# A new order table for attention, norm and the first feature tiles, with 45 dummy products in place of 95

## The chip, the cores and the metric

The kernel runs on one core of a Trainium2 chip. The metric is the device time of one execution, in microseconds (us). The engines are named as in the profile: PE is the tensor engine (PEld its weight loads), DVE the vector engine, ACT the scalar engine, POOL the GpSimd engine, and SP the engine that issues the loads and stores.

## The reference

Three layers follow each other for 2304 tokens (4 batches of 576) of 512 numbers. The attention is linear: q is normalised over each head's 64 numbers, k over all the tokens of its batch.

```python
q_s = np.exp(q - np.max(q, axis=-1, keepdims=True));  q_s = q_s / (np.sum(q_s, axis=-1, keepdims=True) + 1e-09)
k_s = np.exp(k - np.max(k, axis=2, keepdims=True));   k_s = k_s / (np.sum(k_s, axis=2, keepdims=True) + 1e-09)
kv = np.einsum('bhsd,bhse->bhde', k_s, v)             # 4 batches, 8 heads, 576 tokens, 64
x = np.einsum('bhsd,bhde->bhse', q_s, kv)             # then reshaped to 2304 x 512
xn = x / np.sqrt(np.mean(x * x, axis=-1, keepdims=True) + 1e-06) * rms_g
g = xn @ w_gate                                       # 512 -> 1536
x2 = (g / (1.0 + np.exp(-g)) * (xn @ w_val)) @ w_out  # 1536 -> 512
h = x2 @ w_in                                         # 512 -> 2048
y = (np.maximum(h, 0.0) + np.log1p(np.exp(-np.abs(h)))) @ w2_out   # 2048 -> 512
```

The weights of both dense layers arrive as float64 numbers.

## The kernel before

**Tiles and products.** Tokens come in six blocks of 384 (j = 0 to 5), hidden units in feature tiles of 128. Batches are cut into chunks of 128 tokens, three to a block; block 1 holds tokens of batch 0 and batch 1, so its attention output needs both. Each float32 product is three matmuls with float32r halves (`mm3`, L512 to L514: high by high, high by low, low by high), so a gate, value or output tile of one block is 12 matmuls of 384 columns. Each weight tile must first be turned from float64 words into those halves: an absolute value on ACT (CA, L213), a clamp (CL, L218), three bit operations on DVE (CD, L224, L228, L232), a cast on ACT (CC, L241) and a subtraction (CS, L246).

**Stages.** The first dense layer runs in groups of 3, 4 and 5 feature tiles; in a group each block takes its feature tiles one after the other, one *step* each: gate product G, Silu S (L593), value product V, product of both A (L605), its halves AH (L609) and AL (L613), output product O. Steps 0 to 14 are the first group for blocks 0 to 4. They, the attention, the norm and the conversion of the first weights are in the order table. From step 15 on code in loops sets the order; it is the same before and after the change.

**The order table.** `ORDER` is a string of operations. The program runs through it once; each operation emits its instructions to its engine, so each engine takes its share in the order of the table. An engine that waits holds up all that stands behind it on that engine alone. Where an operation can run on several engines, its last letter names one (V is DVE, P is POOL, A is ACT). The names are:

- LQ, LK, LX, LV, LW, LG: loads of q, k, v and the norm's factors; F.n: the load of weight tile n. All are issued by SP.
- K0 (maximum over tokens, L307), K1 (transposition, L315), KM (L321), K2 (spread over the partitions, L329), KS (subtraction, L336), KE (exponential, L341), K3 (products of k and v, PSUM tile `kvp`, L353 and L354), K4 (division, into `kvb`, L360 to L363): batch b, four heads at a time, K3.1.0 being batch 1's first four. K4.1.0 and K4.1.2 give batch 1's `kvb`.
- Q0 (L377), QS (L381), QE (L385), QR (L390 to L392), QM (L398): softmax of q; T (L406) and TC (L414): its transposition on PE and the copy to `qT_t`.
- X0.j.m: attention output of block j, a quarter m (L437); SQ its square (L442), XG its product with the norm's factor (L451, L453), XS sums of squares (L457), X1 (L464), XD (L469), XP (a power, L475) and X2 (L481) the root mean square, spread over the partitions, X3 (L485) the division; HH (L501, L503) and HL (L509) the halves that the gate product takes.
- E: copy of a block's finished output of the group (L564, L566).
- B.n: n *dummy* products (`busy`, L575) of a tile of zeros called `warm`, whose result nobody reads. A call is two records in the trace.

**Banks.** Of PSUM's eight banks, operations of the listed part other than G, V, O and B take spare ones in table order: five at first, two from the first gate product on (`bank`, `give`). A bank comes back when its last reader has been emitted.

Of the kernel before, what the change touches and what calls it, by code (L numbers as in the profile page):

```python
# [26 lines left out]
K0.0.0.1 LQ.0.1 B.2 LW.0 K0.0.1.1 QS.0.0.0.P B.1 QE.0.0.1 B.2 LV.0.4.8 K0.0.2.2 K1.0.0 B.1 QE.0.0.0 B.4 KM.0.0
K1.0.2 QR.0.0.0 K2.0.0 B.1 LQ.0.2 B.2 KM.0.2 QM.0.0.0.P B.1 QR.0.0.1 K2.0.2 B.1 F.3 B.1 T.0 KS.0.0 QM.0.0.1.P F.1
B.1 TC.0.A B.2 F.0 B.1 T.1 Q0.0.1 F.2 KE.0.0 B.3 LQ.1.0 B.1 KS.0.2 B.1 QS.0.1.0.P TC.1.A F.5 K3.0.0 F.4 QS.0.1.1.P
QE.0.1.0 F.7 KE.0.2 B.1 QR.0.1.0 B.1 F.8 B.3 LV.1.0.4 QE.0.1.1 Q0.0.2 K3.0.2 QM.0.1.0.V QS.0.2.0.P QR.0.1.1 T.2 MX.1  # L30
QE.0.2.0 B.1 K4.0.2 B.1 QM.0.1.1.P TC.2.A LK.1.2.2 B.2 CA.1 LX.1 B.1 QR.0.2.0 X0.0.3 CL.1.P F.6 X0.0.2 SQ.0.3 K4.0.0
LK.1.0.2 CA.0 B.2 LV.1.4.8 QM.0.2.0.V XG.0.3.A X0.0.0 SQ.0.2 CL.0.V X0.0.1 CA.3 CD.1.0 XS.0.2.3.P CD.0.0 SQ.0.0 B.1
CL.3.V B.1 SQ.0.1 B.1 CD.1.1 B.1 XG.0.0.A B.1 XS.0.0.1.P LW.1 B.1 Q0.1.0 CA.2 B.2 LQ.1.2 XG.0.2.A B.1 XS.0.0.2.P B.2
XG.0.1.A CL.2.V B.2 CD.1.2 B.1 QS.1.0.0.P X1.0 CD.2.0 CC.1 CD.3.0 B.2 QS.1.0.1.P XD.0 CA.4 B.1 CD.3.1 B.2 CD.0.1 B.2
CL.4.P QE.1.0 B.1 CD.3.2 B.1 LQ.1.1 B.2 CD.0.2 B.1 CC.3 B.2 QR.1.0 CA.7 B.1 XP.0 B.2 CC.0 B.2 CS.1.P CA.8 X2.0
CD.4.0 T.3 X3.0.0 T.4 TC.3.A CS.0.P QM.1.0.0.V B.1 TC.4.A B.2 CD.4.1 T.5 CL.8.P B.1 X3.0.1 B.2 HH.0.0.V B.1 X3.0.2
B.1 HH.0.1.A B.1 HL.0.0.V B.1 HH.0.2.A B.1 X3.0.3 B.1 HL.0.1.P G.0.0 K0.1.2.2 HH.0.3.A HL.0.2.P G.0.1 CA.5 CD.4.2
K1.1.2 HL.0.3.P G.0.2 KM.1.2 CC.4 CD.2.1 K2.1.2 CS.3.P CA.6 G.0.3 K0.1.0.2 V.0 CS.4.P KS.1.2 S.0 CL.6.P K1.1.0 G.1.0
KM.1.0 A.0 G.1.1 CD.2.2 K2.1.0 CL.5.P G.1.2 CD.6.0 KE.1.2 KS.1.0 G.1.3 V.1 CC.2 TC.5.A CD.6.1 CS.2.P AH.0.A Q0.1.2
KE.1.0 K3.1.2 Q0.1.1 QS.1.2.0.P CD.5.0 QS.1.1.0.P CD.6.2 K3.1.0 LV.2.4.8 K4.1.2 S.1 AL.0.V X0.1.2 MX.2 QM.1.0.1.V  # L40
QE.1.2.0 O.0 A.1 LV.2.0.4 CC.6 K4.1.0 AH.1.A CS.6.P SQ.1.2 CD.5.1 XG.1.2.A X0.1.0 CL.7.V CD.5.2 AL.1.P X0.1.3 SQ.1.0
CD.7.0 LK.2.2.2 CC.5 G.2.0 XG.1.0.V LQ.2.0 SQ.1.3 G.2.1 CS.5.P CD.7.1 XG.1.3.A G.2.2 LK.2.0.2 CD.8.0 X0.1.1 LW.2
CD.7.2 XS.1.2.3.P O.1 LX.2 CD.8.1 SQ.1.1 CC.7 QS.1.1.1.V XS.1.0.1.P XG.1.1.A CD.8.2 QE.1.1 CS.7.P XS.1.0.2.V G.2.3
T.6 CC.8 QR.1.1 X1.1 CS.8.P V.2 XD.1 S.2 QM.1.1.0.V XP.1 TC.6.A QM.1.1.1.P T.7 A.2 X2.1 TC.7.A AH.2.V X3.1.0 LQ.2.1
AL.2.P T.8 X3.1.1 TC.8.V O.2 X3.1.2 HH.1.0.V X3.1.3 HH.1.1.A HL.1.0.V HL.1.1.P X0.2.0 HH.1.2.V E.0.0.A E.0.2.V
HH.1.3.A X0.2.1 HL.1.2.V E.0.1.A HL.1.3.V G.3.0 SQ.2.0 SQ.2.1 E.0.3.V G.3.1 XG.2.1.A XS.2.0.1.V G.3.2 XG.2.0.V
X0.2.3 Q0.2.0 G.3.3 SQ.2.3 V.3 XG.2.3.A K0.2.2.2 S.3 QS.2.0.0.P QS.2.0.1.P Q0.2.1 X0.2.2 F.9 K1.2.2 SQ.2.2 G.4.0 A.3
QS.2.1.1.P G.4.1 XG.2.2.V G.4.2 KM.2.2 XS.2.2.3.P G.4.3 K0.2.0.2 QE.2.0 K2.2.2 QS.2.1.0.P V.4 AH.3.A KS.2.2
XS.2.0.2.P S.4 AL.3.V K1.2.0 F.10 X1.2 A.4 O.3 XD.2 KM.2.0 XP.2 QR.2.0 QE.2.1 AH.4.A K2.2.0 CA.9 QR.2.1 G.5.0
QM.2.0.0.P KE.2.2 G.5.1 G.5.2 CL.9.P CA.10 KS.2.0 T.9 G.5.3 V.5 AL.4.V QM.2.0.1.P CL.10.V TC.9.V S.5 QM.2.1.0.P  # L50
LQ.3.0 CD.10.0 O.4 A.5 QR.1.2.0 KE.2.0 QM.2.1.1.V X2.2 K3.2.2 AH.5.A X3.2.0 AL.5.V X3.2.1 LQ.3.1 HH.2.0.V O.5
LV.3.4.8 K4.2.2 HH.2.1.A HL.2.1.P X3.2.2 HL.2.0.V HH.2.2.A X3.2.3 T.10 E.1.2.A G.6.0 HL.2.2.V E.1.1.A QM.1.2.0.P
LK.3.2.2 TC.10.A HH.2.3.V G.6.1 Q0.3.0 T.11 HL.2.3.P K3.2.0 TC.11.V Q0.3.1 X0.3.3 MX.3 LV.3.0.4 QS.3.0.0.V G.6.2
QS.3.1.1.P SQ.3.3 G.6.3 QS.3.0.1.V V.6 CD.10.1 K4.2.0 LW.3 S.6 XG.3.3.V LX.3 X0.3.1 E.1.3.V LK.3.0.2 A.6 X0.3.0
CD.10.2 QE.3.0 G.7.0 E.1.0.V G.7.1 CC.10 QR.3.0 G.7.2 SQ.3.0 G.7.3 SQ.3.1 V.7 AH.6.A XG.3.1.A CS.10.V AL.6.P
XS.3.0.1.V QM.3.0.0.P XG.3.0.V X0.3.2 K0.3.2.2 S.7 T.12 SQ.3.2 O.6 TC.12.A K0.3.0.2 G.8.0 XS.3.2.3.V K1.3.0 A.7
XS.3.0.2.P G.8.1 KM.3.0 AH.7.A G.8.2 XG.3.2.V K2.3.0 AL.7.P G.8.3 KS.3.0 X1.3 QS.3.1.0.P S.8 V.8 XD.3 XP.3 X2.3
KE.3.0 A.8 O.7 X3.3.0 AH.8.V QE.3.1 X3.3.1 AL.8.P CD.9.0 HH.3.0.A X3.3.2 K3.3.0 QR.3.1 O.8 HL.3.0.V X3.3.3 HH.3.1.V
K4.3.0 HH.3.2.A G.9.0 E.2.1.A HL.3.1.V K1.3.2 E.2.3.A T.13 KM.3.2 HH.3.3.A G.9.1 HL.3.2.V E.2.0.A T.14 TC.13.V
E.2.2.A G.9.2 TC.14.A CD.9.1 K2.3.2 HL.3.3.V X0.4.0 KS.3.2 QM.3.0.1.P G.9.3 SQ.4.0 V.9 XG.4.0.V CD.9.2 S.9  # L60
QM.3.1.0.V F.11 X0.4.1 A.9 G.10.0 QM.3.1.1.V G.10.1 KE.3.2 G.10.2 G.10.3 AH.9.A K3.3.2 CC.9 AL.9.P F.12 CS.9.P V.10
K4.3.2 S.10 SQ.4.1 CA.11 XG.4.1.V XS.4.0.1.P CL.11.V X0.4.3 CD.11.0 A.10 X0.4.2 SQ.4.3 CD.11.1 O.9 CA.12 XG.4.3.V
SQ.4.2 CD.11.2 XG.4.2.A XS.4.2.3.P CL.12.V CC.11 F.13 AH.10.V G.11.0 CD.12.0 AL.10.P XS.4.0.2.V G.11.1 CD.12.1
G.11.2 CS.11.P G.11.3 CD.12.2 X1.4 S.11 CC.12 V.11 XD.4 XP.4 F.14 CA.13 CS.12.P X2.4 A.11 T.15 CL.13.P X3.4.0 O.10
AH.11.A X3.4.1 TC.15.A HH.4.0.A X3.4.2 X3.4.3 HL.4.0.P CA.14 T.16 HH.4.1.V CD.13.0 T.17 HH.4.2.A HL.4.1.V AL.11.P
G.12.0 TC.17.A CD.13.1 G.12.1 CL.14.P TC.16.V O.11 CD.13.2 HL.4.2.V CC.13 F.15 HH.4.3.V CD.14.0 X0.5.2 E.3.0.A
CS.13.V E.3.2.A X0.5.3 HL.4.3.V E.3.3.A CD.14.1 SQ.5.2 G.12.2 SQ.5.3 G.12.3 CD.14.2 XG.5.2.A XS.5.2.3.P V.12 S.12
XG.5.3.V CC.14 F.16 E.3.1.A CS.14.V CA.15 G.13.0 A.12 X0.5.0 CL.15.V AH.12.A CD.15.0 X0.5.1 SQ.5.0 AL.12.V G.13.1
CD.15.1 SQ.5.1 O.12 XG.5.0.V XS.5.0.1.P CD.15.2 XS.5.0.2.P XG.5.1.V CC.15 F.17 G.13.2 CS.15.V X1.5 G.13.3 XD.5 XP.5
V.13 S.13 X2.5 A.13 G.14.0 X3.5.0 G.14.1 AH.13.V HH.5.0.A G.14.2 X3.5.1 G.14.3 HL.5.0.P AL.13.V HH.5.1.A V.14 X3.5.2  # L70
# [833 lines left out]
```

## Time and profile before

| | |
|---|---|
| three runs | 974.17, 971.95, 974.18 us |
| median | 974.17 us |
| span of the profiled execution | 970.3 us |
| PE busy in the span | 950.6 us, 98% |
| DVE, ACT, POOL busy | 670.7, 513.5, 206.7 us |
| first gate product (step 0) starts | 48.09 us |
| step 15's first gate product starts | 205.84 us |

The span is the time from the first to the last instruction that the profile shows; the runs' times are some microseconds longer, with what lies around it. Times in the trace count from the start of the span. Busy time of PE is summed from modelled ends of pipelined matmuls and includes the dummy products, so it isn't useful work; starts of matmuls in a row tell what one costs. The granted clock of PE is given as a share of full speed, 1.00 being 2.4 GHz. An average over the span hides that the ordered part, the first fifth, and the rest have different limits; so the table of stretches is the view to begin with.

### The profile page before, as it was taken

The numbers are of one execution on the slowest core, as the hardware profiler recorded it, in microseconds if no ns is written. First come the engines' busy times: TensorE is split into PE (matmuls) and PEld (weight loads), VectorE is DVE, ScalarE is ACT, GpSimd is POOL, SyncE is SP. The second block draws the span as 40 slices with busy tenths as digits, with TensorE's granted clock in tenths as the row PEclk, the third lists the DMA queues.
The fourth block names the chain that finished last, engine by engine and source line by source line (L and its number), as shares of the span: only waits on it lengthen the run. The fifth ranks groups of instructions, "written<-read, shape, count | busy, mean of one in ns | idle before, by whom it ended". The sixth has DMA issues, their size and how long they took to land.

```text
span 970.3 us, 13904 instructions
## 1 busy us (share of the span) xinstructions
PE 950.6 (98%) x5374; PEld 895.4 (92%) x5374; DVE 670.7 (69%) x1160; ACT 513.5 (53%) x1014; POOL 206.7 (21%) x184
## 2 busy tenths in 40 slices
...
DMA packets 64162, 55.42 MB, mean 57 GB/s; under 512 B 25440, under 2 KB 58208, under 8 KB 64096
## 3 DMA queue, kind: packets, MB, share of 16 engines
...
q14 instruction: 24, 0.20, 0.1%
...
## 4 chain that ended last, share of the span: by engine, by line
PE 87%; DVE 8%; ACT 2%; issue 1%; POOL 1%; DMA 1%; SPq 0%; DVEq 0%; ACTq 0%
PE acc L514 11%; PE acc L513 11%; PE acc L512 11%; PE h L514 7%; PE h L512 7%; PE h L513 7%; PE v L512 5%; PE g L512 5%; PE v L514 5%; PE g L514 5%; PE g L513 5%; PE v L513 5%; PE kvp L353 2%; DVE km_t L307 2%; PE kvp L354 1%
## 5 line engine op out<-in xcount | busy, mean ns | idle before, releaser
L509 POOL TENSOR_TENSOR hl<-x,hl 128x384 fp32r<-128x384 f32 x68 | 70.1, 1031 | 618.9 <-ACT hl L501 536.4
L514 PE MATMUL h<-hl,w 128*128 128x384 f32 x384 | 129.5, 337 | 0.0
L512 PE MATMUL h<-hl,w 128*128 128x384 f32 x384 | 129.3, 337 | 0.0
L513 PE MATMUL h<-hl,w 128*128 128x384 f32 x384 | 128.9, 336 | 0.0
L850 DVE SCALAR_TENSOR_TENSOR u<-u,e 128x384 f32<-128x384 f32 x96 | 55.0, 573 | 82.8 <-ACT ln L847 82.8
L514 PE MATMUL acc<-w,hb 128*128 128x512 f32 x279 | 110.6, 397 | 0.2 <-DVE hb L843 0.2
L513 PE MATMUL acc<-w,hb 128*128 128x512 f32 x279 | 110.2, 395 | 0.0
L512 PE MATMUL acc<-w,hb 128*128 128x512 f32 x279 | 108.5, 389 | 0.0
L512 PE MATMUL g<-hl,w 128*128 128x384 f32 x288 | 99.9, 347 | 0.0
L763 DVE TENSOR_TENSOR a<-s,v 128x384 f32<-128x384 f32 x57 | 31.5, 552 | 97.5 <-PE v L514 97.5
L512 PE MATMUL acc<-h,w 128*128 128x384 f32 x288 | 97.3, 338 | 0.0
L513 PE MATMUL g<-hl,w 128*128 128x384 f32 x288 | 96.4, 335 | 0.7 <-DVE hl L509 0.7
L512 PE MATMUL v<-hl,w 128*128 128x384 f32 x288 | 97.0, 337 | 0.0
L514 PE MATMUL v<-hl,w 128*128 128x384 f32 x288 | 96.7, 336 | 0.0
L513 PE MATMUL v<-hl,w 128*128 128x384 f32 x288 | 96.6, 335 | 0.0
L513 PE MATMUL acc<-h,w 128*128 128x384 f32 x288 | 96.4, 335 | 0.0
L514 PE MATMUL g<-hl,w 128*128 128x384 f32 x288 | 96.3, 334 | 0.0
L514 PE MATMUL acc<-h,w 128*128 128x384 f32 x288 | 96.3, 334 | 0.0
L751 ACT ACTIVATE s<-g 128x384 f32<-128x384 f32 x57 | 28.1, 493 | 126.5 <-PE g L514 126.5
L765 ACT CAST h<-a 128x384 fp32r<-128x384 f32 x57 | 29.3, 514 | 116.3 <-DVE a L763 116.3
L837 ACT ACTIVATE e<-h 128x384 f32<-128x384 f32 x96 | 47.1, 490 | 75.6 <-PE h L514 75.2
L512 PEld LDWEIGHTS h<-hl,w 128*128 128x128 f32 x384 | 72.2, 188 | 4.1
...
## 6 DMA issues: line engine op xcount, KB each, us to landing
...
```

What stands on the lines that cost most here:

```text
L307: nc.vector.tensor_reduce(out=km_t[:, hs], in_=k_t[:, hs].rearrange("p h r d -> p h d r"), op=ALU.max, axis=AX.X)
L353: nc.tensor.matmul(out=a, lhsT=k_t[:, h, r, :], rhs=v_t[:, h, r, :], start=(r == 0), stop=False)
L354: nc.tensor.matmul(out=a, lhsT=k_t[:SX, h, R, :], rhs=v_t[:SX, h, R, :], start=False, stop=True)
L509: eng.tensor_tensor(out=t[:, 1], in0=src, in1=t[:, 0].bitcast(F32), op=ALU.subtract)
L512: nc.tensor.matmul(out=ps, lhsT=wh, rhs=xh, start=first, stop=False)
L513: nc.tensor.matmul(out=ps, lhsT=wh, rhs=xl, start=False, stop=False)
L514: nc.tensor.matmul(out=ps, lhsT=wl, rhs=xh, start=False, stop=last)
L751: nc.scalar.activation(out=s, in_=g_ps, func=AF.Silu)
L763: nc.vector.tensor_tensor(out=a, in0=s, in1=v_ps, op=ALU.mult)
L765: nc.scalar.copy(out=h[:, 0], in_=a)
L837: nc.scalar.activation(out=e, in_=ps, func=AF.Abs)
L850: nc.vector.scalar_tensor_tensor(out=u, in0=u, scalar=1.0, in1=e, op0=ALU.subtract, op1=ALU.subtract)
```

## The change

`ORDER` has 705 operations where it had 759; the operations that compute are the same. On each engine they stand in another order, movable ones go to other engines, and 45 dummy calls stand where there were 95. `x0g` no longer takes its bank handle out of the table of handles, so XG may stand ahead of SQ. Comments are gone, which makes line numbers of the code three smaller. Counts of instructions on DVE in the listed part, before and after: clamps L218 9 and 14, normalised q L398 8 and 2, XG L451 12 and 7, sums of squares L457 5 and 8, halves HH L503 9 and 7 and HL L509 14 and 8, AH L609 4 and 7, AL L613 7 and 9, result copies L564 4 and 6. ACT's reloads of its function table are 17 and 9.

```diff
 ORDER = """
-LK.0.1.1 LQ.0.0 MX.0 B.2 MK LK.0.0.1 B.1 LX.0 B.1 MV B.1 LK.0.2.2 B.1 LV.0.0.4 B.4 Q0.0.0 B.2 LG B.1 QS.0.0.1.P
+LQ.0.1 LQ.0.0 LX.0 Q0.0.1 QS.0.1.0.V MK QE.0.1.0 LQ.0.2 MX.0 Q0.0.0 LK.0.2.2 LK.0.1.1 QS.0.0.1.P Q0.0.2 QR.0.1.0
+QE.0.0.1 QS.0.0.0.P QM.0.1.0.P B.26 T.2 QE.0.0.0 LK.0.0.1 F.8 QS.0.1.1.P QR.0.0.1 K0.0.2.2 QR.0.0.0 QE.0.1.1 QR.0.1.1
...
-S.14 HL.5.1.P X3.5.3 O.13 HH.5.2.A A.14 HL.5.2.P HH.5.3.V AH.14.A HL.5.3.V AL.14.V
+HH.5.0.A AL.13.P HH.5.1.A A.14 HL.5.3.P HL.5.0.V CS.14.V HL.5.1.V AH.14.A AL.14.V O.13 F.16 F.17
 """
...
-        ps = xps.pop((j, m))
+        ps = xps[j, m]
```

PE at the start of the program, before; `busy` are the dummies, `qTp` is T's transposition, `kmT` is K1's and `kmb` K2's result:

```order
L575 MATMUL busy_115<-warm_80 128x128 x18
L315 MATMUL kmT_160<-ident_79,km_t_95 128x128 x2
L575 MATMUL busy_115<-warm_80 128x128 x5
L315 MATMUL kmT_171<-ident_79,km_t_95 128x128 x2
L329 MATMUL kmb_178<-ident_79,mx_169 128x128 x2
L575 MATMUL busy_115<-warm_80 128x128 x4
L329 MATMUL kmb_196<-ident_79,mx_187 128x128 x2
```

The same place after the change:

```order
L572 MATMUL busy_141<-warm_80 128x128 x26
L403 MATMUL qTp_168<-ident_79,qn_139 128x128 x4
L572 MATMUL busy_141<-warm_80 128x128 x2
L312 MATMUL kmT_197<-ident_79,km_t_95 128x128 x2
L403 MATMUL qTp_200<-ident_79,qn_192 128x128 x4
...
L326 MATMUL kmb_220<-ident_79,mx_207 128x128 x2
L403 MATMUL qTp_229<-ident_79,qn_205 128x128 x4
...
L312 MATMUL kmT_244<-ident_79,km_t_95 128x128 x2
```

The three transpositions of q in block 0 have moved ahead of and between those of k; more of the dummies stand at the very start and fewer behind.

PE at the first gate product (`g`), before; `ms` is X1, `rsb` X2, `qTp` are T.3 to T.5:

```order
L575 MATMUL busy_115<-warm_80 128x128 x14
L464 MATMUL ms_411<-ones_81,sq_t_97 128x1 x3
L575 MATMUL busy_115<-warm_80 128x128 x19
L481 MATMUL rsb_463<-ident_79,rs_422 128x128 x3
L406 MATMUL qTp_468<-ident_79,qn_330 128x128 x4
L406 MATMUL qTp_474<-ident_79,qn_364 128x128 x4
L575 MATMUL busy_115<-warm_80 128x128 x3
L406 MATMUL qTp_488<-ident_79,qn_481 128x128 x4
L575 MATMUL busy_115<-warm_80 128x128 x9
L512 MATMUL g_514<-hl_498,w_456 128x384
```

After; `kvp_512` is K3.1.2, `kvb0` and `kvb1` belong to batches 0 and 1, `xT` is X0.1.0 and X0.1.1:

```order
L351 MATMUL kvp_512<-v_t_94,k_t_93 64x65
L434 MATMUL xT_533<-qT_t_96,kvb0_98 128x192
L434 MATMUL xT_533<-qT_t_96,kvb1_99 128x192
L434 MATMUL xT_548<-qT_t_96,kvb0_98 128x192
L434 MATMUL xT_548<-qT_t_96,kvb1_99 128x192
L509 MATMUL g_570<-hl_536,w_297 128x384
L510 MATMUL g_570<-hl_536,w_297 128x384
```

Batch 1's K3 and two products of block 1 now stand ahead of the first gate product, where dummies stood; before, K3 of batch 1 came after the value products of step 1.

DVE around the second subtraction KS of batch 2 (`k_t` from `kmb`), before:

```order
L377 TENSOR_REDUCE qm_928<-qh_840 128x16
L605 TENSOR_TENSOR a_942<-s_924,v_909 128x384
L451 TENSOR_SCALAR xn_894<-xT_930,g_sb_83 128x384
L321 TENSOR_REDUCE mx_952<-kmT_934 128x2
L307 TENSOR_REDUCE km_t_95<-k_t_93 128x256
L336 TENSOR_TENSOR k_t_93<-k_t_93,kmb_960 128x1280
```

After; `bits` and `early` are weight tiles in conversion:

```order
L333 TENSOR_TENSOR k_t_93<-k_t_93,kmb_768 128x1280
L215 TENSOR_SCALAR bits_844<-bits_844 128x512
L454 TENSOR_TENSOR sq_t_97<-sq_t_97 128x384
L215 TENSOR_SCALAR bits_744<-bits_744 128x512
L374 TENSOR_REDUCE qm_862<-qh_727 128x16
L215 TENSOR_SCALAR early_434<-early_434 128x512
L221 TENSOR_SCALAR bits_844<-bits_844 128x512
L378 TENSOR_TENSOR qh_727<-qh_727,qm_862 128x8x64
L225 SCALAR_TENSOR_TENSOR bits_844<-raw_692,bits_844 128x512
L466 TENSOR_SCALAR rs_881<-ms_876 128x3
L221 TENSOR_SCALAR bits_744<-bits_744 128x512
L333 TENSOR_TENSOR k_t_93<-k_t_93,kmb_869 128x1280
```

Between the two subtractions of batch 2 now stand conversions of weights; before, batch 2's maxima and products of steps stood there.

## Rows read from the trace of the kernel before

**Rows 1.** Busy time per stretch: PE, PEld, DVE, ACT, POOL, then clock, DMA.

```profile
0.00:48.09 48.09, 42.18 (x326) 38.63 (x327) 36.82 (x66) 20.76 (x35) 28.16 (x31) 0.96 1.03 251
48.09:101.60 53.51, 47.74 (x305) 42.70 (x304) 50.55 (x69) 32.83 (x50) 34.03 (x28) 0.97 0.32 85
101.60:205.84 104.24, 100.31 (x668) 92.62 (x666) 86.81 (x150) 54.96 (x89) 43.32 (x38) 1.00 0.25 69
205.84:560.00 354.16, 354.16 (x2045) 354.16 (x2045) 193.35 (x364) 113.28 (x229) 0.00 (x0) 1.00 0.15 46
```

**Rows 2.** Single matmuls: start, duration, engine, line, tiles; steps 0 and 15.

```profile
48.09 0.43 PE L512 MATMUL g<-hl,w 128*128 128x384 f32 x1
...
205.84 0.33 PE L512 MATMUL g<-hl,w 128*128 128x384 f32 x1
206.01 0.33 PE L513 MATMUL g<-hl,w 128*128 128x384 f32 x1
```

**Rows 3.** Two heads of K3, from the same view.

```profile
60.86 0.68 PE L353 MATMUL kvp<-v_t,k_t 128*64 128x65 f32 x8
...
61.73 0.68 PE L353 MATMUL kvp<-v_t,k_t 128*64 128x65 f32 x8
```

**Rows 4.** K1, T, K2 and X0 between gate products, from the same view.

```profile
153.86 0.38 PE L315 MATMUL kmT<-ident,km_t 128*128 128x128 f32 x2
154.08 0.60 PE L406 MATMUL qTp<-ident,qn 128*128 128x128 f32 x4
154.43 0.42 PE L512 MATMUL g<-hl,w 128*128 128x384 f32 x1
...
156.01 0.61 PE L329 MATMUL kmb<-ident,mx 128*128 128x128 f32 x4
156.45 0.82 PE L437 MATMUL xT<-qT_t,kvb 128*128 128x192 f32 x4
156.97 0.48 PE L512 MATMUL g<-hl,w 128*128 128x384 f32 x1
```

**Rows 5.** X2 ahead of an output product, from the same view.

```profile
144.84 0.83 PE L481 MATMUL rsb<-ident,rs 128*128 128x128 f32 x6
145.42 0.43 PE L512 MATMUL acc<-h,w 128*128 128x384 f32 x1
```

**Rows 6.** Groups to 205.84: count | busy, mean ns | idle before; dummies.

```profile
L575 PE MATMUL busy<-warm 128*128 128x128 f32 x190 | 27.4, 305 | 1.0 <-DVE nhalf L526 1.0
```

**Rows 7.** Chain of waits: ten records of dummies at either clock.

```profile
10.46 2.07 PE busy L575 x10
...
27.44 1.12 PE busy L575 x10
```

**Rows 8.** Single instructions on DVE: its first one with its wait.

```profile
5.63 1.22 DVE L377 TENSOR_REDUCE qm<-qh 128x16 f32<-128x1024 f32 x1 [3.29 <-DMA qh<-in_q_dram]
```

**Rows 9.** Groups to 205.84 on DVE, as in rows 6.

```profile
L307 DVE TENSOR_REDUCE km_t<-k_t 128x256 f32<-128x1280 f32 x7 | 16.8, 2410 | 0.0
...
L336 DVE TENSOR_TENSOR k_t<-k_t,kmb 128x1280 f32<-128x1280 f32 x8 | 11.7, 1468 | 0.3 <-PE kmb L329 0.3
...
L605 DVE TENSOR_TENSOR a<-s,v 128x384 f32<-128x384 f32 x15 | 8.3, 550 | 7.4 <-PE v L514 7.2
...
L360 DVE TENSOR_SCALAR den<-kvp 128x2 f32<-128x2 f32 x8 | 1.3, 157 | 10.9 <-PE kvp L354 10.9
```

**Rows 10.** Groups to 205.84 on ACT and POOL, as in rows 6.

```profile
L246 POOL TENSOR_TENSOR w<-early,w 128x512 fp32r<-128x512 f32 x8 | 12.4, 1564 | 4.9 <-ACT w L241 4.9
...
L593 ACT ACT_TABLE_LOAD x9 | 11.5, 1283 | 3.2 <-PE g L514 3.0
...
L341 ACT ACTIVATE k_t<-k_t 128x1280 f32<-128x1280 f32 x8 | 10.2, 1270 | 1.4 <-DVE k_t L336 1.4
```

**Rows 11.** Two stretches of five microseconds, columns as in rows 1.

```profile
75.00:80.00 5.00, 2.37 (x16) 2.09 (x14) 5.00 (x5) 1.87 (x3) 3.60 (x3) 1.00 0.44 67
80.00:85.00 5.00, 4.63 (x22) 4.57 (x23) 3.53 (x7) 3.05 (x5) 3.67 (x3) 0.71 0.00 0
```

More of the change, by code (lines that the diff above doesn't have):

```diff
@@ L25 @@
 ORDER = """
-LK.0.1.1 LQ.0.0 MX.0 B.2 MK LK.0.0.1 B.1 LX.0 B.1 MV B.1 LK.0.2.2 B.1 LV.0.0.4 B.4 Q0.0.0 B.2 LG B.1 QS.0.0.1.P
[L27 to L70, printed above, removed]
@@ L71 @@
-S.14 HL.5.1.P X3.5.3 O.13 HH.5.2.A A.14 HL.5.2.P HH.5.3.V AH.14.A HL.5.3.V AL.14.V
+LQ.0.1 LQ.0.0 LX.0 Q0.0.1 QS.0.1.0.V MK QE.0.1.0 LQ.0.2 MX.0 Q0.0.0 LK.0.2.2 LK.0.1.1 QS.0.0.1.P Q0.0.2 QR.0.1.0
+QE.0.0.1 QS.0.0.0.P QM.0.1.0.P B.26 T.2 QE.0.0.0 LK.0.0.1 F.8 QS.0.1.1.P QR.0.0.1 K0.0.2.2 QR.0.0.0 QE.0.1.1 QR.0.1.1
+QM.0.0.1.P MV B.2 K1.0.2 T.1 QM.0.0.0.P KM.0.2 LW.0 K0.0.0.1 QS.0.2.0.P F.0 LV.0.0.4 B.2 K2.0.2 QM.0.1.1.P LV.0.4.8
+T.0 CA.8 CA.0 K0.0.1.1 KS.0.2 QE.0.2.0 LQ.1.0 B.2 K1.0.0 F.7 LQ.1.1 KM.0.0 CL.0.P TC.1.V QR.0.2.0 CD.0.0 B.2 K2.0.0
@@ new lines @@
+KE.0.2 TC.2.A CL.8.V KS.0.0 KE.0.0 B.1 K3.0.2 CD.0.1 TC.0.A CD.0.2 QM.0.2.0.P CC.0 K3.0.0 CD.8.0 Q0.1.0 K4.0.2 CD.8.1
+QS.1.0.1.P Q0.1.1 X0.0.2 F.3 K4.0.0 CA.7 F.4 QS.1.0.0.P QE.1.0 B.1 X0.0.0 CA.3 LK.1.0.2 LG SQ.0.2 QR.1.0 LX.1 LK.1.2.2
+CL.3.V CL.7.P X0.0.1 MX.1 CA.4 CD.7.0 SQ.0.1 XG.0.1.A CD.3.0 CL.4.V X0.0.3 CD.3.1 SQ.0.0 F.1 XG.0.3.A CD.4.0
+QM.1.0.1.V XS.0.0.1.P LV.1.0.4 T.3 SQ.0.3 XG.0.2.A XS.0.2.3.P LW.1 K0.1.0.2 LV.1.4.8 B.4 T.4 XS.0.0.2.P B.3 K1.1.0
+TC.4.A K0.1.2.2 B.1 X1.0 CA.1 K1.1.2 QM.1.0.0.P KM.1.0 XD.0 CL.1.V F.5 XG.0.0.A TC.3.A K2.1.0 XP.0 KM.1.2 T.5 K2.1.2
@@ new lines @@
+KS.1.0 X2.0 KE.1.0 QS.1.1.0.P CD.1.0 X3.0.1 QS.1.1.1.P TC.5.A KS.1.2 T.6 X3.0.0 CD.8.2 HH.0.1.A X3.0.3 KE.1.2 CS.0.P
+X3.0.2 F.6 CD.4.1 B.1 K3.1.0 HL.0.1.P CD.1.1 CD.3.2 QE.1.1 CD.1.2 K4.1.0 K3.1.2 X0.1.0 HH.0.0.A HL.0.0.P CA.6 CC.8
+CC.1 HH.0.3.A CL.6.V CD.7.1 X0.1.1 CC.3 LK.2.0.2 K4.1.2 SQ.1.0 CS.1.P SQ.1.1 QR.1.1 HL.0.3.P HH.0.2.A LK.2.2.2 G.0.0
+X0.1.2 SQ.1.2 MX.2 XG.1.2.A G.0.1 LX.2 X0.1.3 HL.0.2.V XG.1.3.A G.0.2 QM.1.1.0.V XS.1.0.1.V CD.4.2 CD.6.0 F.2 XG.1.0.A
+SQ.1.3 T.7 F.9 G.0.3 S.0 V.0 CS.3.V TC.6.A TC.7.A QM.1.1.1.P XS.1.2.3.V XS.1.0.2.P G.1.0 T.8 LQ.2.0 K0.2.0.2 G.1.1
@@ new lines @@
+CD.6.1 TC.8.A CD.7.2 CC.4 X1.1 G.1.2 CC.7 CS.4.P CD.6.2 XD.1 K1.2.0 CC.6 CS.7.P CS.6.P CA.5 G.1.3 A.0 XP.1 KM.2.0 S.1
+X0.2.0 Q0.2.0 CA.2 X0.2.3 F.10 V.1 AH.0.A K0.2.2.2 G.2.0 SQ.2.0 XG.2.0.A K1.2.2 XG.2.3.A SQ.2.3 X2.1 CL.2.V LQ.2.1
+LV.2.0.4 KM.2.2 XG.1.1.V A.1 G.2.1 CD.2.0 X0.2.1 CA.9 SQ.2.1 QS.2.0.0.P X3.1.0 AL.0.P QS.2.0.1.P XG.2.1.A G.2.2 X3.1.1
+XS.2.0.1.V G.2.3 HH.1.0.A CD.2.1 HL.1.0.P HH.1.1.A X3.1.2 X3.1.3 K2.2.0 HL.1.1.V LV.2.4.8 V.2 S.2 G.3.0 X0.2.2 AH.1.A
+HH.1.2.V HH.1.3.V QE.2.0 HL.1.3.P G.3.1 HL.1.2.V SQ.2.2 G.3.2 A.2 QR.2.0 G.3.3 V.3 CD.2.2 XG.2.2.A CS.8.P S.3
@@ new lines @@
+XS.2.2.3.V KS.2.0 QM.2.0.1.P CA.10 G.4.0 CL.10.V CC.2 XS.2.0.2.V T.10 LW.2 TC.10.A CL.9.V Q0.2.1 CL.5.V G.4.1 CD.10.0
+K2.2.2 G.4.2 QS.2.1.1.V X1.2 CD.10.1 XD.2 CD.9.0 CS.2.P KE.2.0 O.0 KS.2.2 QM.2.0.0.P AL.1.V KE.2.2 CD.5.0 CD.5.1
+QS.2.1.0.P G.4.3 CD.5.2 K3.2.0 AH.2.V LQ.3.0 K3.2.2 CD.9.1 A.3 CD.10.2 CD.9.2 V.4 K4.2.0 QE.2.1 AL.2.P CC.5 XP.2
+K4.2.2 S.4 CS.5.P T.9 X2.2 QR.2.1 G.5.0 X3.2.2 X3.2.0 X3.2.1 LK.3.0.2 TC.9.A LQ.1.2 QM.2.1.0.P O.1 Q0.3.0 G.5.1 T.11
+CC.9 G.5.2 MX.3 HH.2.1.A O.2 AH.3.V F.11 HL.2.1.P CS.9.P Q0.1.2 X3.2.3 LX.3 QS.1.2.0.V G.5.3 TC.11.A X0.3.3 HH.2.0.V
```

18 lines of the change are left out of this document (added).

## The prediction

> **What bounds the kernel now.** I read three things in this order: the table of busy time by stretch, the starts of single matmuls, and the groups by line. In the table [rows 1] the tensor engine (PE) is busy for all 354.16 us between 205.84 and 560: from the first product behind the ordered part (step 15) on, it has no gap to lose, and the change touches no instruction there. The part that the order table covers is different. Up to the first gate product at 48.09 [rows 2], PE's busy time is mostly dummy products on the `warm` tile; between 48.09 and 205.84 it shows 47.74 of 53.51 and 100.31 of 104.24 us. So I reduce the question to one number, **when does PE reach the first gate product of step 15, now 205.84** [rows 2]. What this moves, the end of the span moves. The span is 970.3 us, the median of the runs 974.17, so 3.87 us lie around the span; I take them as constant and forecast against 974.17.
>
> **What PE has to do in the ordered part.** Prices are from start to start, because ends are modelled. A matmul of 384 columns takes 0.173 us (205.84 to 206.01, [rows 2]), so a gate or value step of 12 takes 2.08, an output step as much. One head of K3 takes 0.87 (60.86 to 61.73, [rows 3]); a K3 has four, 3.48. From [rows 4]: a pair K1 0.22, a transposition T 0.36, K2 0.44, an X0 product some 0.5. X2 takes 0.58 [rows 5], X1 about the same. Thirty gate and value steps 62.4, fourteen output steps 29.1, eight K3 27.8, and 18 T, 24 X0, K1, K2, X1 and X2 some 30.8 make 150.1 us of useful work, the same before and after. Ahead of the first gate product stand 13.7 of it before (two K3, six T, four X0, X1, X2, K1 and K2 of batch 0) and 23.3 after, since K1, K2 and K3 of batch 1, a seventh T and two X0 of block 1 come ahead. So 136.4 are left behind that product before, 126.8 after. Before spends 205.84 − 48.09 = 157.75 on it: it loses 157.75 − 136.4 = **21.4 us** in waits and half-clock stretches. That loss is what a better order can win, and it is all that it can win.
>
> **Dummy products.** 95 calls become 45 (two records a call: 190 records, [rows 6]). They cost PE 27.4 us of busy time, but stand where it would wait. Ten records took 2.07 us at half clock and 1.12 at full clock [rows 7]. Taken out, they win nothing by themselves; I cost them at nothing as long as the engine that PE waits for, VectorE (DVE) as a rule, is what sets the next product's time. What they may cost is clock: see C.
>
> **The front, to the first gate product.** DVE's first instruction waits for a load, 3.29 us, and starts at 5.63 [rows 8]. After, the q half that it needs is the first load on the SP queue instead of the second; a slot there is some half a microsecond, so I take 5.1. From there to the second half-write of `kvb` for batch 1 (K4.1.0) stand 75 DVE instructions in the new order. Priced each at its form's mean in the trace to 205.84, they sum to 53.1: five `L307` maxima 9.7, four `L336` subtractions 5.9, five `L377` 5.5, the conversions of early weights 15.3, the rest 16.7 (the prices of the first two in [rows 9]). Those means overlap in part: all forms sum to 184.6, while the busy time in [rows 1] is 36.82 + 50.55 + 86.81 = 174.2, a factor of 0.944. So 53.1 × 0.944 = 50.1, and DVE is there at 55.2 if it waits for nothing in between. I take that, since matmuls, exponentials and POOL steps that feed it stand well ahead in the table; DVE did wait in this stretch before, mostly for K3's products (10.9 us over the ordered part, [rows 9]), so the bound above is 5.7 more (48.09 − 5.63 − 36.8 of busy time). The two X0 products of block 1 that come next in PE's order need K4.1.0: 2 × 0.58 = 1.2. The **first gate product comes at 56.4**, 8.3 later than before, with 9.6 more work done. With no loss at all behind it, step 15 would begin at 56.4 + 126.8 = 183.2.
>
> **Waits behind it.** I walked PE's, ACT's, POOL's and DVE's orders against each other with row means. Four places wait. (a) About 2.2 us at gate products of step 0 and X1.1, for K4.1.2, the low halves and a normalised q. (b) 1.5 at step 2's first gate product, which needs weight 6: DVE has finished its bits at 5.1 + 68.1 × 0.944 = 69.4, then an ACT cast, then two POOL subtractions at 1.56 each [rows 10] make 73, PE is there at 71.5. (c) 2.8 around the second K1 of batch 2, X2.1 and step 3's gate. (d) 5 us at K3 of batch 2: its `L336` subtraction stands behind six conversions and ends after 97.1 us of row means, that is 5.1 + 97.1 × 0.944 = 96.7; the exponential takes 1.27 [rows 10]; so K3.2.2 starts near 98.0 where PE is ready at 93. Together 11.5. Behind that the table keeps PE's inputs ahead of it in my walk, blocks 3 to 5 included.
>
> **What the walk can't see.** I add 5 us: about 3 for half clock behind waits, which halves PE's pace for some microseconds, and 2 for POOL and DVE disturbing each other and for DVE waiting on value products, which it did for 7.2 us before [rows 9]. 183.2 + 11.5 + 5 = 199.7, against 205.84: **6.1 us less, 974.17 − 6.1 = 968.0 us**.
>
> **Smaller edits.** DVE gives away six normalisations of q and seven low halves and takes clamps and two result copies; net some 3.4 us less over the ordered part by row means, in the sums above. ACT reloads its function table 9 times where the order had 17; each is 1.28 us [rows 10], 10 us of ACT time, hidden: ACT is busy 108.6 of 205.84 us [rows 1], and only a load directly ahead of a waiting product would count; I take 0 for it, bounds 0 and −3 (the 3.0 us it idled for gate products). POOL gains some 4 us by fewer clamps; it is at 105.5 of 205.84, and counts only where a weight's second half is late, (b). The fetch of weight 16 stands last on SP and waits for a conversion; nothing of the ordered part is behind it, and step 15's tiles are loaded before. The changed line in `x0g` (reading the bank handle without removing it) only permits XG ahead of SQ.
>
> **Rivals.** *B, the losses stay.* The walk sees waits of instructions but not all banks: the ordered part hands out spare banks in table order, two of them behind the first gate product, so a bank is one more thing to wait for. If as much is lost behind the first gate product as now, 21.4, step 15 begins at 183.2 + 21.4 = 204.6: 1.2 less, 973.0. For it: DVE's total work falls only by 3.4. Against it: the waits in (a) to (d) are half of 21.4 and I found no other.
>
> *C, the clock falls, and it is slower.* Now PE is granted only 0.71 of its clock in 80 to 85 us, right behind a stretch where it was busy for 2.37 of 5 us [rows 11], so the clock does fall here when PE has little to do. After the change 9 dummy calls stand between the last X0 product of block 0 and the first gate product, where 45 stood. If the four K3 ahead of it run at 1.2 instead of 2.4 GHz, they take 13.9 us more. DVE has other work beside the first two, so I count half of those as hidden: 13.9 − 3.5 = 10.4, and the first gate product comes at 66.8. With my own losses of 16.5, step 15 begins at 66.8 + 126.8 + 16.5 = 210.1, 4.3 late: 978.4; with the 21.4 of now, 983.3. It decides once the first gate product is later than 205.84 − 126.8 − 16.5 = 62.5. For it: the dummies, 38 records between X1 and X2 alone, were there for this. Against it: a K3 is a dense run of matmuls itself, and PE has more useful work in the front after the change.
>
> The Trainium skill, "TensorE: Matmul & The Clock Gate", section "Why this matters for your kernels", advises against gaps of the tensor engine between bursts of matmuls, as its clock then returns to half; that speaks against taking dummies out, and is rival C. The trace agrees as far as the 0.71 behind the half-idle stretch goes.
>
> *D, the walk as it is.* With no allowance step 15 begins at 194.7, 11.1 less: 963.1. It lies inside the range of the forecast.
>
> **How the numbers follow.** About 0.3%, 2.9 us, is what a measurement of this kernel can tell from no change: faster ends at 971.25, slower begins at 977.1. The forecast with D I give 0.62, B 0.20, C 0.18. A few hundredths of the forecast lie above 971.25 and of C below 977.1, which nearly cancel against B's own spread below: faster 0.63, same 0.20, slower 0.17. The range: below, D's 963.1 and 2 more for ACT's table loads, 961.0; above, over B to the near end of C, 978.5, which leaves out C's far part, about 0.10, and below some 0.07.
>
> **What will show it.** The first gate product near 56 (over 62: C); the start of step 15 near 200; the DVE sum ahead of K4.1.0 without waits of over 3 us; a wait of some 5 us at K3 of batch 2 near 95; the granted clock over 0.9 ahead of the first gate product; and from step 15 on, PE as dense as in [rows 1]. I would be wrong if DVE waits ahead of K4.1.0, if low halves or banks hold up steps 5 to 14, or if anything in the dense part moved.

## The result

| | before | after |
|---|---|---|
| runs | 974.17, 971.95, 974.18, 971.47 us | 965.27, 963.36, 964.65, 964.76 us |
| median | 973.06 us | 964.70 us |
| span of the profiled execution | 970.3 us | 963.5 us |
| first gate product | 48.09 us | 56.08 us |
| step 15's first gate product | 205.84 us | 199.07 us |
| DVE busy up to that | 174.17 us | 168.05 us |

The ratio is 0.9918, with an interval of 0.9903 to 0.9934: the change makes the kernel 0.7 to 1.0% faster. The span became 6.8 us shorter, and step 15 begins 6.77 us sooner, so all of the span's gain lies in the ordered part. The medians differ by 8.4 us; the runs of before lie 2.7 us apart, those of after 1.9.

The table of stretches of the kernel after; as in [rows 1] the columns are the stretch, the busy times of PE, PEld, DVE, ACT and POOL with their instructions, and PE's granted clock, DMA share and GB/s:

```profile
0.00:20.00 20.00, 14.88 (x85) 14.09 (x86) 13.99 (x25) 5.88 (x9) 11.61 (x19) 0.83 1.06 241
20.00:40.00 20.00, 14.21 (x123) 11.21 (x122) 19.57 (x34) 10.88 (x18) 10.36 (x10) 0.99 0.87 233
40.00:56.08 16.08, 15.49 (x124) 13.86 (x125) 14.88 (x23) 8.98 (x15) 8.87 (x8) 0.80 0.58 151
56.08:100.00 43.92, 39.19 (x240) 33.33 (x239) 43.54 (x66) 28.86 (x46) 22.90 (x21) 0.96 0.44 115
100.00:199.07 99.07, 97.68 (x629) 92.96 (x629) 76.07 (x136) 44.59 (x81) 44.98 (x42) 1.00 0.26 69
199.07:560.00 360.93, 360.93 (x2084) 360.93 (x2084) 198.62 (x374) 118.25 (x238) 0.00 (x0) 1.00 0.15 46
```

PE is dense from 199.07 on, as it was from 205.84 on. The new thing is DVE's column: from 20 us to 100 us it is full but for some 2 us. In the first 100 us it is busy for 91.98 us, against 85.77 before:

```profile
0.00:100.00 100.00, 83.78 (x568) 72.49 (x568) 91.98 (x145) 54.59 (x86) 53.74 (x55) 0.91 0.67 170
```

The same stretch of the kernel before:

```profile
0.00:100.00 100.00, 88.33 (x619) 79.73 (x620) 85.77 (x133) 52.02 (x83) 60.59 (x57) 0.97 0.67 166
```

What DVE waited for in that stretch, before (the waiting tile, the releaser, us in total, times, longest; the two longest of seven lines):

```profile
DVE den L360 <- PE kvp L354: 4.2, 2, 4.0
DVE qm L377 <- DMA qh<-in_q_dram: 3.3, 1, 3.3
```

and after (two lines of the program's start, the same in both, left out):

```profile
DVE qm L374 <- DMA qh<-in_q_dram: 2.6, 1, 2.6
DVE qm L374 <- DMA qx<-in_q_dram: 0.9, 1, 0.9
DVE xn L482 <- PE rsb L478: 0.6, 1, 0.6
DVE k_t L333 <- PE kmb L326: 0.5, 1, 0.5
```

The wait for K3's products is gone in that stretch. Between 10 and 90 us the list has two waits of DVE, 1.1 us in all. The chain of waits of the kernel after says the same: from 9.11 to about 90 us it runs over DVE, apart from 40.43 to 47.5 on PE and some 4 us on ACT near 78. Summed over its pieces between 9 and 90 us, DVE has 67.9 us of it and PE 6.5; before, DVE had 26.2 and PE 39.2. Its pieces where it passes to PE (start, us, what):

```profile
88.46 1.33 DVE sq_t L454
89.93 0.80 PE ms L461 x6
90.73 0.28 PE acc L509
```

That isn't for good: from 113.24 to 138.20 us the chain runs over DVE once more, which is busy for nearly all of that stretch. Two pieces of it, a maximum of batch 3 and the subtraction with which it hands over to PE, and then the stretch (columns as above):

```profile
120.97 2.08 DVE km_t L304
136.79 1.41 DVE k_t L333
```

```profile
113.00:138.20 25.20, 23.95 (x145) 22.73 (x143) 24.76 (x36) 15.17 (x24) 13.67 (x13) 1.00 0.24 63
```

### The profile page after: what moved, and what is told of

The parts are those of the page before. It is cut to its first block, busy times and chain, and to the rows that moved or that the text cites. A ratio compares the mean times of both kernels' runs of the same rounds, so it can differ in the third digit from the quotient of the medians.

```text
span 963.5 us, 13678 instructions
## 1 busy us (share of the span) xinstructions
PE 941.8 (98%) x5274; PEld 886.9 (92%) x5274; DVE 665.0 (69%) x1157; ACT 504.9 (52%) x1008; POOL 199.9 (21%) x185
## 4 chain that ended last, share of the span: by engine, by line
PE 86%; DVE 11%; ACT 1%; issue 1%; DMA 1%; SPq 0%; DVEq 0%
PE acc L511 12%; PE acc L510 12%; PE acc L509 11%; PE h L511 7%; PE h L509 7%; PE h L510 7%; PE g L509 5%; PE v L509 5%; PE g L510 5%; PE g L511 5%; PE v L510 5%; PE v L511 5%; DVE km_t L304 2%; PE kvp L350 1%; DVE k_t L333 1%; DVE qs L387 1%
## 5 line engine op out<-in xcount | busy, mean ns | idle before, releaser
L509 PE MATMUL h<-hl,w 128*128 128x384 f32 x384 | 129.3, 337 | 0.0
L509 PE MATMUL acc<-w,hb 128*128 128x512 f32 x279 | 108.5, 389 | 0.0
L509 PE MATMUL g<-hl,w 128*128 128x384 f32 x288 | 100.9, 350 | 0.0
L509 PE MATMUL v<-hl,w 128*128 128x384 f32 x288 | 97.7, 339 | 0.0
L509 PE MATMUL acc<-h,w 128*128 128x384 f32 x288 | 97.5, 338 | 0.0
L509 PEld LDWEIGHTS h<-hl,w 128*128 128x128 f32 x384 | 72.2, 188 | 4.1
```

Source lines behind the costliest of these rows:

```text
L509: nc.tensor.matmul(out=ps, lhsT=wh, rhs=xh, start=first, stop=False)
```

## The experiments

My theory is that VectorE's row of work in the first 90 us (up to X1 of block 2, `ms` in the lines above) sets when PE gets its inputs; the new order keeps VectorE fed there. The limit of 90 us leaves out the piece of the chain from 113 us on. (X1.2 belongs to block 2; the expectations call it batch 2's.) The rivals are that the new sharing among engines is the cause by itself, that dummies and PE's clock are, and that every wait of PE is a loss of its own.

### The two halves of the change alone

The order of after with the engines of before, and the order of before with the engines of after. Of the first, one line for example:

```diff
-G.0.2 QM.1.1.0.V XS.1.0.1.V CD.4.2 CD.6.0
+G.0.2 QM.1.1.0.V XS.1.0.1.P CD.4.2 CD.6.0
```

> The changed order, but every movable operation runs on the engine that it had before the change (101 operations differ). Theory order: VectorE's instructions and PE's products still stand in the new order, so most of the gain stays; VectorE has 2.9 us more work over the ordered part and 1.7 us more ahead of the first gate product: that product at 57 to 59, step 15's first at 200 to 203, about 966 to 970 us. Rival engines: the gain comes from sharing the work out anew, and with the old engines it is gone: 972 us or more, step 15 at 205 or later.

> The order of the kernel before with its 95 dummy calls, but every movable operation on the engine that the change gives it. Theory order: no more than 2.9 us of VectorE work less, in an order that was not made for it: 970 to 976 us, step 15 at 203 to 208, the first gate product near 48. Rival engines: most of the 8 us come, 964 to 967 us.

Measured: 981.3 us for the first (0.9% slower than before, 1.0072 to 1.0108) and 980.7 for the second (1.0066 to 1.0106). Neither theory had this: each half alone loses 8 us against before, and together they win 8. With the old engines the first gate product comes at 60.35, an output product of step 0 waits for a weight's second half on POOL, and step 15 begins at 214.79. With the new engines in the old order PE waits 3.4 us for a normalised q on POOL ahead of the first gate product, which comes at 53.36, and step 15 begins at 216.53. The waits of PE that lead the lists, of the first:

```profile
PE kmT L312 <- DVE km_t L304: 7.2, 2, 5.5
PE acc L511 <- POOL w L243: 4.4, 1, 4.4
```

and of the second, to its first gate product:

```profile
PE qTp L405 <- POOL qn L397: 3.4, 1, 3.4
```

DVE's busy time shows something more. Here are the stretches up to step 15, first of after, then of the second mix:

```profile
0.00:199.07 199.07, 181.46 (x1195) 165.45 (x1196) 168.05 (x280) 99.19 (x167) 98.72 (x96) 0.96 0.47 120
```

```profile
0.00:216.53 216.53, 197.18 (x1294) 180.20 (x1295) 173.46 (x280) 109.75 (x175) 99.69 (x96) 0.95 0.42 110
```

Both have 280 instructions of DVE, on the same engines, and the same forms; in the old order they take 5.4 us longer. So what the same instructions of DVE cost differs with the order. The granted clock up to step 15 differs too: 0.98 before, 0.96 after, 0.94 and 0.95 in the two mixes, so half-clock stretches have a share in their loss that isn't separated from the waits. The two mixes show that order and sharing are needed together; that a fuller row of VectorE is what the 6.8 us come from is read from the chains, and no run added to or took from VectorE's row in the order of before.

### Dummies

The changed kernel without any dummy; the changed kernel with 17 more; the kernel before with about half of each run of its dummies.

```diff
-... XS.0.0.2.P B.3 K1.1.0 TC.4.A ... K2.2.2 G.4.2 QS.2.1.1.V X1.2
+... XS.0.0.2.P B.3 B.13 K1.1.0 TC.4.A ... B.2 K2.2.2 G.4.2 QS.2.1.1.V B.2 X1.2
```

> The changed kernel without its 45 dummy calls. Theory order: VectorE sets the pace up to about 90 us, so a slower PE there costs only what lies on the chain: K3 of batch 0 and the products ahead of the first gate product at half clock, first gate product at 57 to 61, step 15 at 200 to 203, 965 to 969 us. Rival clock: PE at half clock sets the front, first gate product over 62.5, 970 us or more.

> The changed kernel with 17 dummy calls more: 13 ahead of K1.1.0, where PE waits 3.9 us and then runs at 0.50 of its clock, 2 ahead of K2.2.2 and 2 ahead of X1.2, where it waits 0.6 and 0.5 us and the output product behind runs at 0.66. Theory order with VectorE as the bound: the first spot gives at most the 1.06 us that VectorE waited there (44.3 and 47.0), the second up to 1.6 us: 962 to 964.5 us, first gate product 55 to 56. Rival clock: the whole 3.2 us of the first spot and the 1.6 come back: under 961 us. If dummies only delay: 965 or more.

> The kernel before, in its own order and with its own engines, with 45 dummy calls in place of 95, each run of them cut by about half. Theory order: dummies only fill waits of PE; fewer of them cost clock behind the waits in the front, 0 to 3 us: 972.5 to 975.5 us. Rival dummies delay: they stand in the way of real products and taking half of them out is a gain of more than 2 us: 970.5 us or less.

Measured: 966.45 us without dummies (interval of the ratio to before 0.9917 to 0.9953); the first gate product comes at 57.93, 1.85 later than in after, and step 15 1.81 later. With 17 more 963.18 (0.9890 to 0.9921), first gate product 54.68, step 15 at 196.84. Before with 45 calls stays where it was: 972.64, ratio 1.0005 (0.9996 to 1.0014). So going from 95 to 45 has no price by itself in the order of before. In the changed kernel all 45 are worth 1.8 us by the medians, and the 17 give 1.5, but both intervals overlap that of after (0.9903 to 0.9934); in the profiled executions it is 1.8 and 2.2 us of span. Two stretches of after:

```profile
40.00:44.00 4.00, 3.46 (x16) 3.33 (x17) 3.79 (x6) 1.14 (x3) 1.79 (x2) 0.50 0.85 155
...
90.00:95.00 5.00, 5.00 (x22) 4.75 (x23) 5.00 (x9) 0.24 (x1) 1.16 (x1) 0.66 0.36 105
```

and the same with 17 dummies more:

```profile
40.00:44.00 4.00, 3.31 (x30) 3.06 (x29) 3.90 (x6) 1.63 (x3) 2.65 (x4) 1.00 1.01 176
...
90.00:95.00 5.00, 4.30 (x40) 3.70 (x38) 5.00 (x9) 0.61 (x1) 1.07 (x1) 1.00 0.27 82
```

With the dummies the granted clock is 1.00 in both. At the first place the first gate product comes 1.4 us sooner; VectorE had only short waits there. Of this gain not all is sure: after and two kernels of the next sections that differ from it only further on have that product at 56.08, 56.20 and 57.10 in their traces; this kernel and two that differ from it only further on have it at 54.68, 54.78 and 56.34. At the second place the output product of step 0, which took 3.71 us (90.59 to 94.30) at 1.2 GHz, goes at 2.4 GHz.

### PE's waits against VectorE's row

Two operations move on VectorE, meant to end PE's two longest waits behind the first gate product, with no work added or removed.

```diff
-HH.0.3.A CL.6.V CD.7.1 X0.1.1 CC.3 LK.2.0.2 K4.1.2 ... QR.1.1 HL.0.3.P ... X0.1.3 HL.0.2.V
+HH.0.3.A K4.1.2 CL.6.V CD.7.1 X0.1.1 CC.3 LK.2.0.2 ... HL.0.3.P ... X0.1.3 HL.0.2.V QR.1.1
```

> The changed kernel with two operations moved on VectorE alone: K4.1.2 ahead of two conversions (CL.6, CD.7.1), and QR.1.1 behind the low half HL.0.2. VectorE does the same work; PE's two longest waits right behind the first gate product (X0.1.2 2.0 us and G.0.2 1.7 us too long) should go. Theory VectorE chain: VectorE works without a gap up to X1 of batch 2 at 90 us, so the 3.7 us that PE gains are given back ahead of that place: 963.7 to 965.5 us, within 1 us of the changed kernel, X1.2 at 89 to 90.5. Rival PE waits: each wait of PE removed is time gained: 961 to 962 us, step 15 near 195.5.

Then a maximum over tokens is done twice, once in batch 1 (near 38 us), once in batch 3 (near 119).

```diff
-XS.0.0.1.P LV.1.0.4 T.3 SQ.0.3 XG.0.2.A XS.0.2.3.P LW.1 K0.1.0.2
+XS.0.0.1.P LV.1.0.4 T.3 SQ.0.3 XG.0.2.A XS.0.2.3.P LW.1 K0.1.0.2 K0.1.0.2
```

> The changed kernel with one maximum of batch 1 (K0.1.0.2, 2.4 us on VectorE, starting near 38) done twice; the result is the same. Theory VectorE chain: the first gate product moves by 2.0 to 2.6 us to some 58.4 and step 15 by as much, to some 201.4: 966.5 to 967.3 us. Rival PE waits: it is partly hidden, under 1 us: 964.7 to 965.7 us.

> The changed kernel with one maximum of batch 3 (K0.3.0.2, 2.4 us on VectorE, near 119 to 121) done twice. Behind 95 us PE is nearly dense and VectorE has gaps. Theory VectorE chain up to 95 only: hidden but for 0 to 0.8 us: 964.5 to 965.5 us. If VectorE sets the pace here too: 966.5 to 967.3 us.

Measured: the first, 964.31 us, is within 0.4 of after. The edit ended one of the two waits, 1.7 us at X0.1.2; the other, for T.7's q, grew from 0.9 to 1.7. PE still reached V.0 at 62.65, 1.0 us sooner than in after (with the first gate product 0.7 later), but X1 of block 2 at 89.77, where after has 89.93: what PE had gained was given back there. Step 15 begins 0.96 us sooner; that was won behind X1 of block 2, where this execution was granted 1.00 of the clock in 90 to 95 us. The second, 967.55, is 2.85 more; the first gate product moves from 56.08 to 58.76, X1 of block 2 to 92.60, step 15 to 200.95. Both speak for VectorE's row up to 90 us, and against PE's waits as losses of their own. The third speaks against a limit to 90 us: it costs 2.5 us, at 967.21, where I expected under 0.8. In its trace step 15 is 2.33 us late, of which 0.69 was there at X1 of block 2 already, with the same code up to there. PE waits for the doubled maximum:

```profile
125.88 0.41 PE L312 MATMUL kmT<-ident,km_t 128*128 128x128 f32 x2 [2.11 <-DVE km_t L304]
```

In after that transposition starts without a wait, but the maximum had ended just ahead of it:

```profile
123.76 0.38 PE L312 MATMUL kmT<-ident,km_t 128*128 128x128 f32 x2
```

So a place with no wait in the trace need not have slack. VectorE is full there too, and this maximum is the piece at 120.97 us of the chain shown above, which runs on to T.13's wait at 138.33. What was wrong was my limit of 90 us, and that VectorE has gaps behind it: between 113 and 138 us it has next to none.

### Taking work from VectorE

If VectorE's row is the bound, less of it should help: four operations ahead of X1 of block 2 go to POOL where POOL is idle.

```diff
-QM.1.1.0.V ... CS.3.V TC.6.A TC.7.A QM.1.1.1.P ... XS.2.0.1.V ... XS.2.0.2.V
+QM.1.1.0.P ... TC.6.A TC.7.A QM.1.1.1.P CS.3.P ... XS.2.0.1.P ... XS.2.0.2.P
```

> The changed kernel with four operations of VectorE handed to POOL where POOL is idle: QM.1.1.0 (1.53 us on VectorE), CS.3 (0.68), XS.2.0.1 (0.55) and XS.2.0.2 (1.40); all stand ahead of X1 of batch 2. Theory VectorE chain: X1.2 comes 2 to 3.5 us sooner, near 87, and step 15 1 to 2.5 us sooner (other places bind behind it): 962 to 963.8 us. If something else than VectorE's amount of work sets X1.2, or POOL is too slow for it: 964.5 us or more.

Measured: 967.93 us in the median, 3.2 more than after, where 0.9 to 2.7 less was expected. Its twelve runs lie in two groups: six between 965.18 and 966.33, with 0.989 to 0.991 of the clock granted over the span (after has 0.989 to 0.993), and six between 969.54 and 972.4, with 0.981 to 0.986. So only about 1.3 us of the loss stand at the clock of after; the rest goes with a lower clock, and there is no trace of such a run. The profiled execution, 965.86, is of the first group: step 15 begins at 199.65, 0.58 later than in after, and X1 of block 2 starts at 90.25, no sooner. VectorE's instructions in after from 62.44 on (start, us):

```profile
62.44 0.55 DVE L454 TENSOR_TENSOR sq_t<-sq_t 128x384 f32<-128x384 f32 x1
62.91 0.68 DVE L229 SCALAR_TENSOR_TENSOR early<-early 128x512 int32<-128x512 int32 x1
63.51 0.41 DVE L221 TENSOR_SCALAR early<-early 128x512 int32<-128x512 int32 x1
```

and the same three in this kernel, with POOL beside them:

```profile
61.10 1.40 DVE L454 TENSOR_TENSOR sq_t<-sq_t 128x384 f32<-128x384 f32 x1
62.42 1.53 DVE L229 SCALAR_TENSOR_TENSOR early<-early 128x512 int32<-128x512 int32 x1
63.88 1.52 DVE L221 TENSOR_SCALAR early<-early 128x512 int32<-128x512 int32 x1
```

```profile
60.94 2.46 POOL L395 TENSOR_TENSOR qn<-qh,qs 128x512 f32<-128x512 f32 x2 [2.90 <-PE xT L434]
63.37 1.74 POOL L243 TENSOR_TENSOR w<-early,w 128x512 fp32r<-128x512 f32 x1
```

Three instructions that took 1.64 us take 4.45 while POOL does, among other things, the first two of the operations that VectorE was rid of; those had taken 2.21 us on VectorE. Near 77 us VectorE also waits 1.5 us for K1 of batch 2, which it doesn't in after. Up to step 15 VectorE has four instructions fewer, 4.2 us by their durations in after, and is busy for 167.80 us instead of 168.05: almost all of it came back as longer instructions. The Trainium skill, "SBUF — State Buffer", section "SBUF: two separate sides", says that the two engines share a pair of ports as an exclusive lock: where a GpSimd instruction meets a VectorE instruction in a two-port mode, or, if it reads SBUF, one with two inputs in SBUF, the one that starts first holds the pair for its whole instruction and the other blocks. The three durations agree with it: each instruction ends 0.3 to 0.6 us behind the end of one on POOL (at 62.08, 63.40 and 65.11). The third has one input only, and no run here shows its mode.

### One more wait, and all together

In after, T.13 waits ahead of V.8 for a bank that VectorE reads:

```profile
138.33 0.63 PE L403 MATMUL qTp<-ident,qn 128*128 128x128 f32 x4 [1.39 <-DVE k_t L333]
```

To the kernel with 17 dummies more I added the exchange of T.13 and V.8, and then also the four operations on POOL.

```diff
-T.13 X3.3.1 CA.13 E.1.0.A CL.13.P QE.3.1 V.8
+X3.3.1 CA.13 E.1.0.A CL.13.P QE.3.1 V.8 T.13
```

> The kernel with 17 dummies more (963.2 us), and T.13 behind V.8 instead of ahead of it on PE: T.13 waits 1.4 us for a bank until VectorE's subtraction for batch 3 has read it, and V.8 could run in that time. Theory bank wait is a loss of its own: step 15 1.0 to 1.5 us sooner, 961.5 to 962.5 us. If PE only waits elsewhere instead: 963 us or more.

> The changed kernel with 17 dummies more, T.13 behind V.8, and the four operations handed from VectorE to POOL together. If the three gains add: 959.5 to 961.5 us. If they share one limit: 962 us or more.

Measured: 962.83 us with the exchange (0.9891 to 0.9916), the fastest of all, and 967.21 with the four operations besides (0.9933 to 0.9967). The exchange gives 0.35 us in the median, less than its runs scatter; in the profiled executions step 15 begins 1.4 us sooner, but 1.1 of that was there at X1 of block 2, ahead of the exchange. VectorE is gone from the chain between 95 us and step 15, which now runs over PE, and yet little is won. That the bank's wait is a loss of its own stays open. The kernel with everything has three runs between 964.97 and 965.75, at 0.991 of the clock, and three between 968.67 and 970.62, at 0.984 to 0.989; either group is slower than the exchange alone, so the gains don't add. Its profiled execution is the slowest of the six. There step 15 begins at 204.13, 8.7 us later than with the exchange alone (195.46), but only 2.3 of this was there at X1 of block 2. The other 6.4 come between X1 of block 2 and of block 3, where it ran at 1.2 GHz; first this kernel, then that with the exchange alone:

```profile
96.00:110.00 14.00, 14.00 (x80) 12.41 (x81) 8.54 (x21) 4.61 (x5) 5.45 (x5) 0.51 0.49 134
```

```profile
96.00:110.00 14.00, 14.00 (x100) 13.26 (x100) 12.27 (x27) 5.27 (x10) 10.18 (x10) 1.00 1.03 227
```

So its loss in the trace is mostly clock. What the four operations have to do with the longer half-clock stretches wasn't tested.

## Why the prediction was right, point by point

- **The first gate product**: forecast 56.4, measured 56.08. VectorE's second half-write of batch 1's `kvb` ended at 55.08, forecast 55.2. Row means times 0.944 carried it; my assumption of no wait in between was 2.0 us too kind (0.9 for the rests of q, 0.5 and 0.6 in K and the norm), and the priced work, 50.1, took 55.08 − 4.96 − 2.0 = 48.1. That the two errors cancel was luck.

The write (L360, two halves), in VectorE's row of after:

```profile
54.49 0.59 DVE L360 TENSOR_TENSOR kvb<-kvp,den 64x128 f32<-64x128 f32 x2
```

- **The loss behind it**: forecast 16.5 us over the 126.8 of useful work, measured 199.07 − 56.08 − 126.8 = 16.2. The sum was right, the places partly. (a) was 3.7 (X0.1.2 2.0 and G.0.2 with T.7 1.7 too long) for 2.2; (b) 0.3 for 1.5, and not at step 2's first gate product, which starts at 73.06 without a wait; (c) 1.7 for 2.8. (d) was right in time and wrong in place: the exponential ended at 97.1 and K3's second half began at 98.40, forecast 98.0, but PE didn't wait there. It had lost its time ahead, at K2 of batch 2, at X1 of block 2 and at 1.2 GHz in the output product of step 0, and reached K3 only at 94.94. The wait at T.13, 1.4, I didn't see. The places that I can name come to about 10 us; the other 6 are in waits and prices that I didn't take apart, where the forecast had 5 for what the walk can't see. So that the sum came within 0.3 us is partly luck. What the traces list as waits of PE behind the first gate product fell from 9.7 us to 5.7, most of the 5.2 by which the loss fell.

```profile
98.40 0.39 PE L350 MATMUL kvp<-v_t,k_t 128*64 128x65 f32 x3
```

```profile
95.81 1.27 ACT L338 ACTIVATE k_t<-k_t 128x1280 f32<-128x1280 f32 x1 [5.57 <-DVE k_t L333]
```

- **Step 15**: forecast 199.7, measured 199.07. The dense part didn't move.
- **The base** was the weak step. Of what lies around the span I said 3.87 us, the median minus the span. In after's runs it is 1.75 to 1.77. So the profiled execution of before took about 972.1, if the same lies around it, not 974.17; 6.1 less is 966.0, where the profiled one of after took 965.27. From the median I came to 968.0, 3.3 too high.
- **VectorE's work**: I said 3.4 us less, by counts and row means; it was 6.1 less. The term was mis-sized, as I held each instruction's length fixed: the second mix has the new counts in the old order and takes 173.46, only 0.7 less than before, and the new order takes 5.4 off that.
- **Sharing and order** I treated as separate edits whose sums add. The two mixes show that they don't: each alone is 8 us slower than before.
- **Rival C** was there and small. Ahead of the first gate product the granted clock was 0.88, where I had written over 0.9: it was 0.83 in the first 20 us and 0.50 in 40 to 44. But batch 1's K3 ran at full rate (6.92 us for both; 6.96 by the price from before), and the dummies put back gave at most 1.4 us there, where C took 10.4. C's price was too high besides: at 1.2 GHz a head of K3 took 1.47 us in the kernel with everything (97.61 to 99.08), where C counted twice 0.87.
- **Rival B** was wrong: the loss behind the first gate product is 16.2, not 21.4.
